# Three loads, a table and a rotation put in another order in a fused SSM and SwiGLU kernel

## The chip, the cores and the metric

The kernel runs on one core of a Trainium2 chip. A core has five engines with an instruction stream each: TensorE (PE in the profile; PEld is its weight load), VectorE (DVE), ScalarE (ACT), GpSimd (POOL) and SyncE (SP). They meet through semaphores only. Transfers between the chip's memory (DRAM) and the core's on-chip memory are made by 16 DMA engines; a transfer is issued from the queue of SP, ACT or POOL. The metric is the device time of one execution in microseconds (us), lower is better; "the time before" is the median of several runs.

## What is computed

One input x of 2048 rows by 512 columns (bf16) is normalised row by row, and the normalised x feeds two branches whose results are added to x:

```python
xn = layernorm(x)                                  # (2048, 512)
# branch A: a diagonal complex state space model
Lam_bar = exp(dt * Lam);  B_bar = ((Lam_bar - 1) / Lam)[:, None] * B
Bu = xn @ B_bar.T                                  # (2048, 512) complex
h[t] = Lam_bar * h[t-1] + Bu[t]                    # 2048 steps
yA = 2 * real(h @ C.T) + xn * Dskip
# branch B: a gated feed-forward layer, F = 1376
yB = (silu(xn @ w_gate) * (xn @ w_up)) @ w_down
out = x + yA + yB
```

## The kernel before

The 2048 rows are four chunks of 512 (`NCH`), each of four row tiles of 128 (`TPC`). Everything that TensorE multiplies needs x transposed, so a row tile is normalised in `xall` (the last chunk in `xn_end`) and transposed into `xnT`, for the first two row tiles on TensorE (`xT_pe`), for all others by a DMA transpose on SP's queue (`xT_dma`, L226).

The recurrence with complex coefficients is turned into a real one: the input of each chunk is rotated by an angle that grows with the time step (forward rotation, `rotation(..., False)`, L362), a real scan with decay `r_t` runs over it on VectorE (L400, eight scans a chunk), and the result is rotated back. The rotations multiply by two tables, cosine `c16` and sine `s16`, that the kernel makes itself: `table_ops` (L256) makes for each pair of the four 128-state groups the angles (`turns`), the sine's argument and the cosine's argument (`half`, on VectorE), and the two sines (`sine`, L278, on ScalarE). One rotation is six VectorE instructions over 2048 elements a row: f1 real part times cosine, f2 real part times sine, f3 imaginary part times sine, f4 their sum, f5 imaginary part times cosine, f6 the second sum. Its products lie in a pool of three buffers, `pm`, that the tables use too.

TensorE's order is fixed by the program. A head works on the first chunk's weight columns 0 to 5 row tile by row tile, as they come (`head_mm`, L635, in PSUM banks `held`, then `second`); `head_out` (L641) takes each finished pair of column groups through Silu and a copy on ScalarE, and a product on VectorE (L648). Then come column groups 6 and 7 (L433), which need the fourth weight group `wg3`, `wu3`; the first chunk's B projection (L358), which needs the transposed B (`BT`); groups 8 to 10; and for each later chunk its B projection, its gate and up products, and its output matmuls (L529, L536, L546).

VectorE's and ScalarE's side work is put in a list with prices by hand (`queue`), and `pump(us)` takes from the list after each piece of TensorE's work as much as the price allows; `need(tag)` takes until a tag is used up. So a changed price or place in the list shifts where every later side operation stands among the others. `multiply(keep)` issues the products that are waiting. `ln_rest(c)` (L612) is the later chunks' normalisation: four statistics (L182, L183), then `ve` (L191, VectorE), `rstd` (L192, a power on POOL), `nb` (L195) where ScalarE norms, and the four norms, each followed by its transpose.

The weights of the gate and the up projection are in five groups, each one transfer for the gate and one for the up (L112). Groups 0 to 2 are issued at the start from SP and ACT. `wg3` and `wu3` are issued from ACT behind the last `rstd_act` of the first chunk (L687, L688). `load_mid` (L135) follows on SP behind the first chunk's last transpose: the second chunk's x, eight transposes of B, the fifth weight group. `load_late` (L147) comes on SP behind the second chunk's transposes: `wu_last`, x of the third and fourth chunk, the down weights `wd_sb`. Later on SP: eight transposes of C (`CT`, L819), the third chunk's transposes, and L827, which copies x of the first three chunks to the output in DRAM; POOL adds the results onto it (L513, L557).

`params_a`, `params_a2` and `params_sin` (L246 to L306) make small per-state parameters on VectorE and ScalarE. `params_b` (L308) is a series of small multiplies on POOL.

Of the kernel before, what the change touches and what calls it, by code (L numbers as in the profile page):

```python
# [23 lines left out]
def kernel(  # L24
# [17 lines left out]
    nc = tc.nc  # L42
# [6 lines left out]
    NT = L // 128  # L49
    NCH = L // CW  # L50
    TPC = CW // 128
# [24 lines left out]
    def flat(ap3):  # L76
        return ap3.rearrange("p q j -> p (q j)")

    x_v = A_x[0].rearrange("(n p) d -> p n d", p=128)
    out_v = out[0].rearrange("(n p) d -> p n d", p=128)  # L80
    wg_v = B_w_gate.rearrange("(k p) f -> p k f", p=128)
    wu_v = B_w_up.rearrange("(k p) f -> p k f", p=128)


    xall = const.tile([128, NT, D], BF16, name="xall")
# [3 lines left out]
    wg_g, wu_g = [], []  # L89
# [6 lines left out]
    wd_sb = const.tile([128, FT, D], BF16, name="wd_sb")  # L96
# [7 lines left out]
    def wslice(groups, fi, k):  # L104
        for (a, b), t in zip(fgroups, groups):
            if a <= fi < b:
                return t[:, k, (fi - a) * 128:(fi - a) * 128 + fsz[fi]]


    def load_w1(q, tiles, view, gi):  # L110
        a, b = fgroups[gi]
        q.dma_start(out=tiles[gi][:], in_=view[:, :, a * 128:min(F, b * 128)])  # L112
# [20 lines left out]
        nc.gpsimd.dma_start(out=prm_rows[i * NQ:(i + 1) * NQ, :], in_=v.rearrange("(q j) -> q j", j=128))  # L133

    def load_mid():  # L135
        nc.sync.dma_start(out=xall[:, TPC:2 * TPC, :], in_=x_v[:, TPC:2 * TPC, :])
        for part, src in enumerate((A_B_re, A_B_im)):
            for k in range(KD):
                nc.sync.dma_start_transpose(out=BT[:, part, k, :], in_=src[:, k * 128:(k + 1) * 128])
        load_w1(nc.sync, wg_g, wg_v, 4)  # L140
        load_w1(nc.sync, wu_g, wu_v, 4)
# [3 lines left out]
        nc.gpsimd.dma_start(out=w_last[:, :, LB + LA:128], in_=wu_v[:, :, FL + LB:F])  # L145

    def load_late():  # L147
        nc.sync.dma_start(out=wu_last[:], in_=wu_v[:, :, FL:FL + LB])
        nc.sync.dma_start(out=xall[:, 2 * TPC:NT, :], in_=x_v[:, 2 * TPC:NT, :])
        nc.sync.dma_start(out=wd_sb[:, 0:nfull, :], in_=B_w_down[0:nfull * 128, :].rearrange("(k p) d -> p k d", p=128))  # L150
        if nfull < FT:
            nc.sync.dma_start(out=wd_sb[0:F - FL, nfull, :], in_=B_w_down[FL:F, :])

    nfull = F // 128
# [69 lines left out]
    def xT_dma(n):  # L224
        c, i = divmod(n, TPC)
        nc.sync.dma_start_transpose(out=xnT[:, :, n * 128:(n + 1) * 128], in_=xn_tile(c)[:, i, :])  # L226
# [62 lines left out]
    def tt(o, a, b, op):  # L289
        V.tensor_tensor(out=o, in0=a, in1=b, op=op)  # L290

    def params_sin():

        def turns(dst, shift):
            src = ws2[:]
            if shift:
                V.tensor_scalar(out=dst[:], in0=src, scalar1=shift, scalar2=None, op0=ALU.add)
                src = dst[:]
            V.tensor_scalar(out=kk[:], in0=src, scalar1=MAGIC, scalar2=MAGIC, op0=ALU.add, op1=ALU.subtract)
            tt(dst[:], src, kk[:], ALU.subtract)  # L300

        V.tensor_scalar(out=ws2[:, 1, :], in0=ws2[:, 0, :], scalar1=float(CW), scalar2=None, op0=ALU.mult)
        turns(fs1, 0.0)
        nc.scalar.activation(out=sin1[:], in_=fs1[:], func=ACT.Sin, scale=TWO_PI_LO)
        turns(fc1, 0.25)
        nc.scalar.activation(out=cos1[:], in_=fc1[:], func=ACT.Sin, scale=TWO_PI_LO)  # L306
# [55 lines left out]
    def rotation(src, dst, back):  # L362

        box = {}

        def mul(i, tab):
            t = ssm.tile([128, W], BF16, name="pm", bufs=3)
            V.tensor_tensor(out=t[:], in0=flat(src()[:, i]), in1=flat(tab[:]), op=ALU.mult)  # L368
            return t

        def f1():
            box[0] = mul(0, c16)
        def f2():
            box[1] = mul(0, s16)
        def f3():
            box[2] = mul(1, s16)
        def f4():
            V.tensor_tensor(out=flat(dst()[:, 0]), in0=box[0][:], in1=box[2][:], op=ALU.subtract if back else ALU.add)
        def f5():
            box[3] = mul(1, c16)  # L380
        def f6():
            V.tensor_tensor(out=flat(dst()[:, 1]), in0=box[3][:], in1=box[1][:], op=ALU.add if back else ALU.subtract)
        return [(1.15, f) for f in (f1, f2, f3, f4, f5, f6)]

    def ssm_ops(c):

# [49 lines left out]
    def gu_tile(c):  # L436
        if c not in gu_tiles:
            gu_tiles[c] = gut.tile([128, FT - 1, CW], BF16, name="guT")
        return gu_tiles[c]
# [125 lines left out]
    def queue(tag, ops, at=None):  # L565
        ops = [[op[0], op[1], op[2] if len(op) > 2 else None, tag] for op in ops]
        if at is None:
            backlog.extend(ops)
        else:
            backlog[at:at] = ops  # L570
# [58 lines left out]
    def head_mm(sets, fis, which, lo, hi, ks=range(KD)):  # L629

        base = lo * 128 // HALF * HALF
        for fi in fis:
            p, j = place[fi]
            for k in ks:
                nc.tensor.matmul(sets[p][which][:, j, lo * 128 - base:hi * 128 - base],  # L635
                                 lhsT=wslice((wg_g, wu_g)[which], fi, k),
                                 rhs=xnT[:, k, lo * 128:hi * 128], start=(k == 0), stop=(k == KD - 1))

    def head_out(sets, p, half):

        if half == 0:  # L641
            head_u[p] = up_p.tile([128, 2, CW], BF16, name="u2")
        cols = slice(half * HALF, (half + 1) * HALF)
        a, b = pairs[p]
        g, u = gu_tile(0)[:, a:b + 1:b - a, cols], head_u[p][:, :, cols]
        nc.scalar.activation(out=g, in_=sets[p][0][:], func=ACT.Silu)
        nc.scalar.copy(out=u, in_=sets[p][1][:])
        products.append(lambda: V.tensor_tensor(out=g, in0=g, in1=u, op=ALU.mult))  # L648
# [35 lines left out]
    rstd_act(3)  # L684
    norm_dve(3)
    xT_dma(3)
    load_w1(nc.scalar, wg_g, wg_v, 3)  # L687
    load_w1(nc.scalar, wu_g, wu_v, 3)  # L688
    load_mid()
    head_mm(held, (0, 1), 0, 1, 2, kh[0])  # L690
    head_mm(held, (0, 1), 1, 1, 2, kh[0])
# [4 lines left out]
    head_mm(held, (2, 3), 1, 0, 2)  # L696
    params_a(pp)
    params_a2()
    params_sin()
    head_mm(held, (4, 5), 0, 0, 2)  # L700
    head_mm(held, (4, 5), 1, 0, 2)
    tables = table_ops()
    stats1, norm1 = ln_rest(1, False)
    queue("tables", tables[:1])
    queue("ln1", stats1 + [(0.0, load_w_last)])
    queue("tables", tables[1:2])
    queue("ln1", norm1)
    queue("tables", tables[2:])
    second = []

    def more():
# [1 line left out]

    more()
    head_out(held, 0, 0)
    head_mm(second, pairs[0], 0, 2, 3)
    head_mm(second, pairs[0], 1, 2, 3)
    pump(GU / 2)
# [83 lines left out]
            multiply(0 if q else 1)  # L802
    fwd0, back0 = ssm_ops(0)
    stats2, norm2 = ln_rest(2, True)
    queue("ssm0", fwd0[0:2] + [(1.5, params_b)] + fwd0[2:6])
    stats3, norm3 = ln_rest(3, True)
    queue("ln2", stats2)
    queue("ssm0", fwd0[6:8])
    spread(fwd0[8:] + back0, norm2 + stats3 + norm3, "ssm0",
           ["ln2"] * len(norm2) + ["ln3"] * (len(stats3) + len(norm3)))  # L810
    queue("cf", c_ops())
# [12 lines left out]
    gateup_chunk(1)  # L824
    nc.gpsimd.dma_start(out=dsk_bc[:], in_=A_Dskip.partition_broadcast(128))
    bproj_chunk(2)
    nc.sync.dma_start(out=out[0, 0:(NT - TPC) * 128, :], in_=A_x[0, 0:(NT - TPC) * 128, :])  # L827
    queue_ssm(2)
    out_chunk(0)
    gateup_chunk(2)  # L830
# [40 lines left out]
```

## Time and profile before

| what | value |
|---|---|
| runs | 180.29, 180.37, 180.94 us; median 180.37 |
| the profiled execution's own time | 180.51 us |
| its span, from the first instruction to the last | 178.7 us |
| granted TensorE clock | 0.999 |
| DMA | 15.80 MB, mean 88 GB/s over the span |
| TensorE, matmuls of the gate and up projection (L433) | 34.6 and 34.3 us |
| TensorE, output matmuls (L529, L546) | 36.7 and 28.0 us |
| TensorE, B projection (L358) | 28.3 us |
| VectorE, scans (L400) | 24, mean 1261 ns |
| statistics of VectorE (L182), idle before them for x | 3.4 us |

The page cuts the span in 40 equal slices. A digit is a busy share in tenths:

```
PE   8989999999999999999999999999999999999992
DVE  6847998699999977999999999999999999990032
ACT  3489669988599649923966662013766600220000
DMA  5999497997366602200360000005569500162012
```

TensorE's row is full from the second slice to the last but one; the DMA engines are full in slices 2 to 8 and again later. Times in the timeline count from the span's start. A row of the timeline gives start, duration, engine, line, operation, output, inputs, shape and count, and in brackets how long the engine stood idle before it and what ended the wait. An engine with a q (SPq, ACTq) is the issue of a transfer, not the transfer.

### The profile page before, as it was taken

How to read it: one execution, taken by the hardware profiler on the slowest of the kernel's cores; microseconds unless marked ns; L12 is line 12 of the kernel's file. 1: busy time of each engine (PE TensorE's matmuls, PEld its weight loads, DVE VectorE, ACT ScalarE, POOL GpSimd, SP SyncE). 2: the span in 40 equal slices, each digit the busy share in tenths (PEclk: the TensorE clock that was granted, in tenths of full speed). 3: DMA queues.
4: the chain of work that ended last, by engine and by line, in shares of the span. 5: the costliest groups of instructions: out<-in, count | busy, mean ns of one | idle time of the engine just before them, and what ended most of it. 6: DMA issues, size and time to landing. Idle time of an engine off the chain costs nothing.

```text
span 178.7 us, 2511 instructions
## 1 busy us (share of the span) xinstructions
PE 172.8 (97%) x925; PEld 85.2 (48%) x940; DVE 152.8 (86%) x224; ACT 96.0 (54%) x172; POOL 35.7 (20%) x48
## 2 busy tenths in 40 slices
PE   8989999999999999999999999999999999999992
PEld 2879444444443444444444444444444444444752
DVE  6847998699999977999999999999999999990032
ACT  3489669988599649923966662013766600220000
POOL 6000596081500040000710000004180000150000
PEclk9999999999999999999999999999999999999999
DMA  5999497997366602200360000005569500162012
GB/s 161 302 261 158 92 199 102 254 326 157 75 75 182 231 0 59 58 4 0 39 78 0 2 4 0 0 0 59 59 94 182 82 0 0 4 86 34 0 59 59
DMA packets 30284, 15.80 MB, mean 88 GB/s; under 512 B 17904, under 2 KB 30176, under 8 KB 30240
## 3 DMA queue, kind: packets, MB, share of 16 engines
q1 hardware_dynamic: 22320, 9.97, 25.5%
q0 software_dynamic: 3536, 3.41, 14.6%
q10 hardware_dynamic: 4416, 2.26, 4.8%
q8 instruction: 7, 0.11, 0.3%
q14 instruction: 5, 0.04, 0.1%
HBM read 8.03 MB, written 5.24 MB: 74 GB/s over the span
## 4 chain that ended last, share of the span: by engine, by line
PE 78%; DVE 9%; DMA 5%; ACT 4%; issue 2%
PE ps L433 23%; PE ps L529 19%; PE ps L546 15%; PE ps L358 12%; DMA xnT<-xall 4%; PE ps L635 4%; DVE pm L368 3%; PE ps L536 2%; DVE g L400 2%; DVE stats L182 2%; DMA xall<-in_A_x_dram 1%; ACT u L448 1%; PE ps L473 1%; ACT guT L447 1%; PE ps L484 1%
## 5 line engine op out<-in xcount | busy, mean ns | idle before, releaser
L529 PE MATMUL ps<-wd_sb,guT 128*128 128x512 bf16 (+2 forms) x177 | 36.7, 355 | 0.2
L433 PE MATMUL ps<-xnT,wg 128*128 128x512 bf16 x134 | 34.6, 379 | 0.2
L433 PE MATMUL ps<-xnT,wu 128*128 128x512 bf16 x133 | 34.3, 379 | 0.1
L400 DVE TENSOR_TENSOR_SCAN g<-r_t,car,u 128x512 bf16<-128x512 f32 x24 | 28.7, 1261 | 0.0
L358 PE MATMUL ps<-xnT,BT 128*128 128x512 bf16 x126 | 28.3, 379 | 0.4 <-DMA xnT<-xall 0.3
L546 PE MATMUL ps<-CF,wt 128*128 128x512 bf16 (+2 forms) x141 | 28.0, 355 | 0.2
L557 POOL DMA_DIRECT2D out_dram<-res x12 | 10.6, 1048 | 76.4 <-ACT res L556 76.4
L529 PEld LDWEIGHTS <-guT 128*128 128x128 bf16 x180 | 16.9, 98 | 18.0
L447 ACT ACTIVATE guT<-ps 128x512 bf16<-128x512 f32 x34 | 20.4, 601 | 5.8 <-PE ps L433 5.7
L448 ACT CAST u<-ps 128x512 bf16<-128x512 f32 x34 | 20.1, 590 | 6.4 <-PE ps L433 6.4
L360 ACT CAST u<-ps 128x512 bf16<-128x512 f32 x32 | 18.2, 589 | 7.3 <-PE ps L358 7.3
L556 ACT CAST res<-ps 128x512 bf16<-128x512 f32 x12 | 6.7, 594 | 28.1 <-PE ps L546 27.0
L433 PEld LDWEIGHTS <-wu 128*128 128x128 bf16 x136 | 13.3, 98 | 16.0
L433 PEld LDWEIGHTS <-wg 128*128 128x128 bf16 x136 | 13.3, 98 | 15.8
L546 PEld LDWEIGHTS <-wt 128*128 128x128 bf16 x144 | 13.4, 98 | 14.4 <-DVE CF L344 0.4
L358 PEld LDWEIGHTS <-BT 128*128 128x128 bf16 x128 | 12.4, 98 | 15.8 <-issue 0.8
L549 DVE TENSOR_TENSOR res<-ps,xn_end 128x512 bf16<-128x512 f32 (+2 forms) x6 | 3.0, 514 | 11.9 <-PE ps L546 11.9
L192 POOL TENSOR_TENSOR rstd<-ve,neg_half 128x4 f32<-128x4 f32 x3 | 5.3, 1760 | 37.0 <-DVE ve L191 37.0
L182 DVE BATCH_NORM_STATS2 stats<-xall 128x6 f32<-128x512 bf16 x14 | 9.5, 678 | 3.4 <-DMA xall<-in_A_x_dram 3.4
L452 DVE TENSOR_TENSOR guT<-guT,u 128x1024 bf16<-128x1024 bf16 x17 | 11.4, 675 | 0.0
L368 DVE TENSOR_TENSOR pm<-u,c 128x2048 bf16<-128x2048 bf16 x8 | 9.8, 1222 | 1.5 <-ACT c L278 1.4
L368 DVE TENSOR_TENSOR pm<-g,c 128x2048 bf16<-128x2048 bf16 x8 | 9.7, 1215 | 0.1
(114 smaller groups left out, 194.2 us busy)
## 6 DMA issues: line engine op xcount, KB each, us to landing
out_dram<-in_A_x_dram SPq DMA_DIRECT2D x1, 1536.0 KB, 6.9
out_dram<-res POOLq DMA_DIRECT2D x12, 128.0 KB, 3.1
out_dram<-xall POOLq DMA_DIRECT2D x3, 512.0 KB, 9.3
wd_sb<-in_B_w_down_dram SPq DMA_DIRECT2D x1, 1280.0 KB, 9.9
wu<-in_B_w_up_dram ACTq DMA_DIRECT2D x4, 256.0 KB, 4.5
xall<-in_A_x_dram SPq DMA_DIRECT2D x1, 1024.0 KB, 6.7
wg<-in_B_w_gate_dram ACTq DMA_DIRECT2D x3, 256.0 KB, 4.7
wg<-in_B_w_gate_dram SPq DMA_DIRECT2D x2, 256.0 KB, 4.0
```

The source lines that it names most:

```text
L182: nc.vector.bn_stats(out=stats[:, n, :], in_=xall[:, n, :])
L358: nc.tensor.matmul(ps[:], lhsT=BT[:, part, k, q * 128:(q + 1) * 128], rhs=xnT[:, k, c * CW:(c + 1) * CW], start=(k == 0), stop=(k == KD - 1))
L360: nc.scalar.copy(out=u_tiles[c][:, part, q, :], in_=ps[:])
L368: V.tensor_tensor(out=t[:], in0=flat(src()[:, i]), in1=flat(tab[:]), op=ALU.mult)
L400: V.tensor_tensor_scan(out=g()[:, part, q, :], data0=r_t[:, q:q + 1].to_broadcast([128, CW]), data1=u_tiles[c][:, part, q, :], initial=ini ...
L433: nc.tensor.matmul(ps[:fs, lo:hi], lhsT=wslice(groups, fi, k), rhs=xnT[:, k, c * CW + lo:c * CW + hi], start=(k == 0), stop=(k == KD - 1))
L447: nc.scalar.activation(out=guT[:fs, fi, :], in_=psg[:fs], func=ACT.Silu)
L448: nc.scalar.copy(out=u_pair[c][:fs, fi % 2, :], in_=psu[:fs])
L452: products.append(lambda: V.tensor_tensor(out=g, in0=g, in1=u, op=ALU.mult))
L529: nc.tensor.matmul(o[:], lhsT=gu_tiles[c][:, fi, i * 128:(i + 1) * 128], rhs=wd_sb[:, fi, lo:hi], start=(fi == 0), stop=False)
L546: nc.tensor.matmul(o[:], lhsT=w_tiles[c][:, part, q, i * 128:(i + 1) * 128], rhs=CF[:, part, q, lo:hi], start=False, stop=(c > 0 and part ...
L557: nc.gpsimd.dma_start(out=out_v[:, n, :], in_=res[:], accum_op=ALU.add)
```

## The change

- `wg3` and `wu3` are issued from POOL instead of ACT. Ahead of them VectorE sets two elements of `wg3` to zero, behind the first chunk's last norm; as the load overwrites them, POOL has to wait for it.
- The second chunk's x is issued from POOL behind those two, instead of from SP ahead of B's transposes.
- In `load_late` x of the third and fourth chunk goes ahead of `wu_last`, and the large part of `wd_sb` is two transfers.
- A forward rotation issues f2, f3, f1, f4, f5, f6; the backward one is unchanged.
- `params_sin` moves behind the first `head_out`. On VectorE its instructions stay where they were, on ScalarE its two sines come behind that Silu and copy.
- In the list, the sine's argument of the first state pair (`tables[1]`) comes ahead of the second chunk's statistics, and the cosine's (`tables[2]`) ahead of its norms.
- In the list, the third chunk's statistics come after f4 of the first chunk's rotation, instead of after f6. The price of `params_b` goes from 1.5 to 0.1.
- The copy of x to the output is two transfers. As the list is used up sooner, the fourth chunk's transposes stand ahead of it on SP.

```diff
     def load_mid():
-        nc.sync.dma_start(out=xall[:, TPC:2 * TPC, :], in_=x_v[:, TPC:2 * TPC, :])
         for part, src in enumerate((A_B_re, A_B_im)):
...
     def load_late():
+        nc.sync.dma_start(out=xall[:, 2 * TPC:NT, :], in_=x_v[:, 2 * TPC:NT, :])
         nc.sync.dma_start(out=wu_last[:], in_=wu_v[:, :, FL:FL + LB])
-        nc.sync.dma_start(out=xall[:, 2 * TPC:NT, :], in_=x_v[:, 2 * TPC:NT, :])
-        nc.sync.dma_start(out=wd_sb[:, 0:nfull, :], in_=B_w_down[0:nfull * 128, :].rearrange("(k p) d -> p k d", p=128))
+        wd_v = B_w_down[0:nfull * 128, :].rearrange("(k p) d -> p k d", p=128)
+        for a, b in ((0, 5), (5, nfull)):
+            nc.sync.dma_start(out=wd_sb[:, a:b, :], in_=wd_v[:, a:b, :])
...
-        return [(1.15, f) for f in (f1, f2, f3, f4, f5, f6)]
+        return [(1.15, f) for f in ((f1, f2, f3, f4, f5, f6) if back else (f2, f3, f1, f4, f5, f6))]
...
     xT_dma(3)
-    load_w1(nc.scalar, wg_g, wg_v, 3)
-    load_w1(nc.scalar, wu_g, wu_v, 3)
+    nc.vector.memset(wg_g[3][:, 0, 0:2], 0.0)
+    load_w1(nc.gpsimd, wg_g, wg_v, 3)
+    load_w1(nc.gpsimd, wu_g, wu_v, 3)
+    nc.gpsimd.dma_start(out=xall[:, TPC:2 * TPC, :], in_=x_v[:, TPC:2 * TPC, :])
     load_mid()
...
     params_a2()
-    params_sin()
     head_mm(held, (4, 5), 0, 0, 2)
...
-    queue("tables", tables[:1])
+    queue("tables", tables[:2])
     queue("ln1", stats1 + [(0.0, load_w_last)])
-    queue("tables", tables[1:2])
+    queue("tables", tables[2:3])
     queue("ln1", norm1)
-    queue("tables", tables[2:])
+    queue("tables", tables[3:])
...
     head_out(held, 0, 0)
+    params_sin()
     head_mm(second, pairs[0], 0, 2, 3)
...
-    queue("ssm0", fwd0[0:2] + [(1.5, params_b)] + fwd0[2:6])
+    queue("ssm0", fwd0[0:2] + [(0.1, params_b)] + fwd0[2:4])
     stats3, norm3 = ln_rest(3, True)
     queue("ln2", stats2)
-    queue("ssm0", fwd0[6:8])
+    queue("ssm0", fwd0[4:8])
...
-    nc.sync.dma_start(out=out[0, 0:(NT - TPC) * 128, :], in_=A_x[0, 0:(NT - TPC) * 128, :])
+    for a, b in ((0, TPC * 128), (TPC * 128, (NT - TPC) * 128)):
+        nc.sync.dma_start(out=out[0, a:b, :], in_=A_x[0, a:b, :])
```

## The prediction

> **What bounds the kernel now.** First the page's busy shares.
>
> ```profile
> span 178.7 us, 2511 instructions
> PE 172.8 (97%) x925; PEld 85.2 (48%) x940; DVE 152.8 (86%) x224; ACT 96.0 (54%) x172; POOL 35.7 (20%) x48
> ```
>
> TensorE (PE) has work almost throughout; the profiled execution took 180.51 us, 1.8 us of it outside the span. So a change that removes no matmul can gain only what PE stands still. Next, therefore, PE's own waits:
>
> ```profile
> PE ps L635 <- DMA xnT<-xall: 0.8, 1, 0.8
> PE ps L358 <- DMA xnT<-xall: 0.3, 1, 0.3
> ```
>
> Both are for transposed x. The waits understate the loss, since a matmul's modelled end runs past the slot in which the next can start. So I took slots from the timeline. First stretch:
>
> ```profile
> 7.83 2.62 SPq L226 DMA_TRANSPOSE xnT<-xall  x2
> 8.17 0.41 ACTq L112 DMA_DIRECT2D wg<-in_B_w_gate_dram  x1
> 8.62 0.68 ACTq L112 DMA_DIRECT2D wu<-in_B_w_up_dram  x1
> ...
> 10.20 1.04 PE L635 MATMUL ps<-xnT,wu 128*128 128x256 bf16 x8
> ...
> 10.50 0.58 SPq L136 DMA_DIRECT2D xall<-in_A_x_dram  x1
> ...
> 11.99 0.62 PE L635 MATMUL ps<-xnT,wg 128*128 128x128 bf16 x8 [0.75 <-DMA xnT<-xall]
> ```
>
> The eight 256-column matmuls of 9.33 hand over at 10.20: 0.109 each. The eight of 10.20 are thus through at 11.07, and the next start at 11.99: **0.92 lost**. They wait for row tile 2, whose transpose was issued at 7.83 and landed 4.1 later. What the DMA engines did meanwhile, in the queue view of 10.5 to 11.7:
>
> ```profile
> q10 hardware_dynamic: 643, 0.32, 110.5%
> q1 hardware_dynamic: 32, 0.00, 1.6%
> ```
>
> q10 is ScalarE's queue, q1 SyncE's: the fourth weight group, issued at 8.17 and 8.62, had the engines nearly to itself while PE waited for q1. Second stretch:
>
> ```profile
> 48.59 0.14 DVE L195 SCALAR_TENSOR_TENSOR nb<-mv,rstd 128x4 f32<-128x4 f32 x1
> ...
> 48.76 0.81 ACT L205 ACTIVATE xall<-xall,nb,rstd 128x512 bf16<-128x512 bf16 x1 [1.20 <-DVE nb L195]
> ...
> 56.27 1.03 PE L433 MATMUL ps<-xnT,wu 128*128 128x512 bf16 x4
> ...
> 57.62 4.69 PE L358 MATMUL ps<-xnT,BT 128*128 128x512 bf16 x20 [0.32 <-DMA xnT<-xall]
> ```
>
> 512 columns take 0.216 a slot (32 in 6.9 in stage L358), so the four of 56.27 are through at 57.13: **0.49 lost** at 57.62. This goes back through the transpose and the norms on ScalarE to `nb` of the third chunk on VectorE, late because VectorE was idle earlier:
>
> ```profile
> 14.59 0.69 DVE L182 BATCH_NORM_STATS2 stats<-xall 128x6 f32<-128x512 bf16 x1 [2.88 <-DMA xall<-in_A_x_dram]
> ...
> 21.23 0.85 POOL L144 DMA_DIRECT2D w_last<-in_B_w_gate_dram  x1
> 21.87 1.12 DVE L200 TENSOR_SCALAR xall<-xall,mv,rstd 128x512 bf16<-128x512 bf16 x3
> 22.09 0.80 POOL L145 DMA_DIRECT2D w_last<-in_B_w_up_dram  x1
> ...
> 33.95 1.23 DVE L368 TENSOR_TENSOR pm<-u,c 128x2048 bf16<-128x2048 bf16 x1 [1.36 <-ACT c L278]
> ```
>
> From 58 on PE is closed up. At most some 1.4 us is to be had, plus a few hundredths between stages.
>
> **The change, part by part.** *Hold and POOL issue.* The memset (row: 128x4 memset, 0.06) follows the last first-chunk norm, which ends at 8.81, so POOL issues from about 8.9. The nearest rows, `w_last` with as many rows per transfer, took 0.85 and 0.80 each; the far ones, the skip stores, 1.30 to 1.65. I take 0.85, the same kind of load: wg3 at 8.9, wu3 at 9.75, the second chunk's x at 10.6. From issue to landing 256 KB took 3.5 to 4.9 on the other queues; POOL's 512 KB accumulating stores took 5.6 to 10.8. SP's 512 KB x took 4.1, and POOL's small `w_last` (3.4) stood 1.2 over SP's `wu_last` (2.2). So wg3 is there by 14, wu3 by 15.5 (PE wants them at 17.32 and 18.18, less 0.92), and x at 10.6+4.1+1.2 = 15.9; bounds 14.7 and 21.4.
>
> *Tile 2 and 3 transposes.* Without q10's load a transpose lands 2.45 (the last chunk's four) to 2.8 (the median of BT's imaginary half) after issue: tile 2 at 10.3 to 10.65, wanted at 11.07. The 0.92 goes. PE then wants tile 3 sixteen plus sixteen short matmuls later, at 11.07+32x0.056 = 12.86. Issued at 9.25, it lands at 11.7 clean. Beside POOL's 128 KB of `w_last`, the last BT transpose took 3.6: 12.9, a wait of 0.04. I take none, since POOL's first data can come only about 1.9 after 8.9 (an estimate from `w_last`: issued 21.23, the engines' software queue first busy about 23.1).
>
> *ScalarE* is rid of 0.41+0.68 of issuing; `dt_t` (9.34) starts when prm is there, about 9.05, and the table load ends at 11.0, not 11.28. With the two small sines (0.21, 0.19) put behind the first Silu and copy, those run 11.0 to 12.06. This matters: the second pair reuses their banks at 11.07+0.88 = 11.95 and 12.39. At the old times (12.08, 12.55) it would have cost 0.16.
>
> *VectorE.* The half of the sine table (0.69+1.23) moves ahead of the second chunk's statistics and fills the 2.88 idle. But as built, five products stand ahead of the first statistics, and the fifth needs ScalarE's copy of the fifth pair, about 16.3 (before, less 0.2). So: product to 16.65, four statistics at 0.80 to 19.9, product 20.3, half of the cosine table (0.69+0.72+1.22) to 23.05, product 23.7, four norms at 0.37 to 25.2. x at 15.9 is hidden behind that product with 0.75 to spare. Before, the norms ran 21.87 to 23.91, so **this chain is later**, not earlier. SP loses one issue (0.58), passes BT and the fifth weights by 23.1, and issues the four transposes at 24.1 and 1.3 apart: the last at 28.0 instead of 27.74, landing at 30.5 to 30.8 (2.45 to 2.8). PE wants it at 32.09-0.92 = 31.17. The row of 3.6 would make it 31.6; I charge 0.1 for that. The last BT transpose came at 24.91 when wanted at 24.87; it is issued 0.6 or more sooner and no longer beside `w_last`: nothing.
>
> *Sine first.* The sine is ready at 32.97 before, 0.92 sooner now as it follows PE's pace on ScalarE: the rotation starts at 32.05 instead of 33.95, and the cosine multiply, third, never waits. With f5 and f6 behind the third chunk's statistics, `ve` comes at about 40.7 (45.14) and `nb`, behind f5, f6 and three scans, at 46.7 (48.59). The norms stand one weight pair sooner on ScalarE, 1.67 apart: the last ends about 52.5, its transpose lands at 55.0; PE wants it at 57.13-0.92 = 56.2. The 0.49 goes. x of chunks three and four, issued behind the transposes at 29.4 without `wu_last` (0.57) ahead, lands 6.7 later at 36.1; the statistics want it at 37.4.
>
> *The rest.* wd_sb in two: one more SP issue (0.58), so CT's transposes end at 46.9 instead of 46.3; the next transpose wants SP at 47.4. The output copy in two: it now stands behind the fourth chunk's transposes, issued about 71 instead of 56.30, landed (6.9) by 79; POOL's first accumulation onto it is at 86.18. Were that gone, it would still be off PE's path. params_b's smaller price only moves the order. What is late next: the fourth chunk's last transpose landed at 73.98 with PE there at 74.3; PE being 1.4 sooner, it must be 1.1 sooner; VectorE is 1.9 ahead since the rotation, so nothing, and the C factors behind them likewise.
>
> *Sum*, against 180.51: -0.92 -0.49 +0.10 = -1.31, so 179.2. The runs' median, 180.37, is 0.14 below that execution: **179.1 us**.
>
> **Rivals.** (A) *The second chunk's transposes take over.* For: the chain above is the later one by its own rows, margin 0.4 to 0.7. If VectorE reaches the norms 1.4 us later than I reckon, PE waits about 0.9 at stage L358: gain 0.5, 179.9. Against: every step before them has a row.
>
> (B) *Tile 2 stays late.* The third weight group's second half, still on ScalarE's queue, landed only at 9.84. If that and not the fourth group held the transpose, the 0.92 stays and only 0.49 goes: 179.9. Against: 110% of q10 between 10.5 and 11.7, when the third group had landed.
>
> (C) *POOL's loads come late (slower side).* If POOL's issues stall beside VectorE, which is busy 8.9 to 11.4 and 12.1 to 14.3, wg3 goes out about 11.5, wu3 14.4 to 15.5, x at 16.5, landing near 20. The statistics begin 3.3 later than 16.7, the last transpose lands at 33.8: PE starts the second B projection 1.7 later than before, and the third chunk, 3 later on VectorE, gains nothing: 182.1. It decides when x lands after 16.7 + (32.1-30.8) = 18.0. For: POOL's small multiplies took 0.20 to 1.21 for the same shape. Against: L145 took 0.80 beside three norms of VectorE, no longer than the 0.86 of the output stores that POOL issues singly.
> By the Trainium skill, SBUF — State Buffer, section "SBUF: two separate sides", a VectorE operation in a two-port mode locks GpSimd out of writing descriptors, and a POOL-issued DMA of 620 ns becomes 3100. By that figure the three issues would cost an estimated 7.4 us more and x would land beyond 22. The trace does not bear it out at 21.87 to 22.99, but shows it beside no table arithmetic.
>
> **How the numbers follow.** Forecast 0.58, A 0.15, B 0.13, C 0.12, the rest scattered (0.02). About 0.5% (0.9 us) is what a measurement of this kernel tells from no change: faster is under 179.47. The forecast is nearly all there; A and B fall within; C is slower. Faster 0.60, same 0.28, slower 0.12. Low end 178.6: 1.4 plus the few tenths between stages near 73 and 75 (0.09 and 0.10) and the spread of the runs. High end 180.7 takes in A and B; C's 182.1 stays out.
>
> **What would show it.** Right: no PE wait near 11, tile 2 landed under 11; the last transpose of chunk two before PE; the first rotation near 32; no PE wait at stage L358 for chunk three. Wrong: statistics of chunk two idle on x past 16.7 (C), a wait of PE for `xnT` near 31 (A) or still near 11 (B).

## The result and the profile after

| what | before | after |
|---|---|---|
| runs, median (lowest to highest), us | 180.81 (180.29 to 183.2), 6 runs | 182.05 (181.59 to 182.61), 6 runs |
| ratio to before, 95% interval | | 1.0072 [1.0045, 1.0099] |
| the profiled execution's own time, us | 180.51 | 182.61 |
| its span, us | 178.7 | 180.8 |

Ratios, here and below, compare fast runs alone, and the medians below are theirs: of the six runs before, 183.2 stays out (the other five have a median of 180.69), and so do four, four and one of twelve runs in three kernels below (183.2 to 184.6 us, at a granted clock of 0.987 to 0.991).

The change made the kernel slower by 0.7%. Forecast was 179.1.

TensorE's waits after, from the view of waits; the columns are the sum in us, the number of waits and the longest:

```profile
PE ps L359 <- DMA xnT<-xall: 1.8, 1, 1.8
PE ps L359 <- DMA BT<-in_A_B_re_dram: 0.6, 1, 0.6
PE ps L636 <- DMA xnT<-xall: 0.5, 1, 0.5
```

Three new waits stand where two were, all of them for transfers. Their places, from the timeline after:

```profile
8.15 2.62 SPq L227 DMA_TRANSPOSE xnT<-xall  x2
9.45 0.82 POOL L112 DMA_DIRECT2D wg<-in_B_w_gate_dram  x1 [5.32 <-DVE prm L248]
10.27 0.77 POOL L112 DMA_DIRECT2D wu<-in_B_w_up_dram  x1
11.04 0.75 POOL L691 DMA_DIRECT2D xall<-in_A_x_dram  x1
11.43 0.61 PE L636 MATMUL ps<-xnT,wg 128*128 128x128 bf16 x8
13.89 0.61 PE L636 MATMUL ps<-xnT,wg 128*128 128x128 bf16 x8 [0.51 <-DMA xnT<-xall]
20.54 0.69 DVE L183 BATCH_NORM_STATS2 stats<-xall 128x6 f32<-128x512 bf16 x1 [3.49 <-DMA xall<-in_A_x_dram]
22.05 2.18 PE L359 MATMUL ps<-xnT,BT 128*128 128x512 bf16 x8 [0.58 <-DMA BT<-in_A_B_re_dram]
35.12 1.24 PE L359 MATMUL ps<-xnT,BT 128*128 128x512 bf16 x5 [1.83 <-DMA xnT<-xall]
```

Row tile 2 is on time: its matmuls start at 11.43 with no wait. Row tile 3 is not (13.89). VectorE stands 3.49 for the second chunk's x and begins its statistics at 20.54, 3.9 later than the prediction had them; the transposed B comes late (22.05); and the second chunk's transposes, which follow those statistics, hold TensorE until 35.12. Counted in slots as in the prediction, TensorE loses 0.67 at tile 3, 0.74 and 0.28 for B, 1.99 at chunk two: 3.68, where before lost 0.92, 0.09 (at 24.7) and 0.49. That is 2.2 more; the two profiled executions differ by 2.1 (the one after was 0.36 later from the start and won some 0.4 back behind the third chunk). How long the transfers took, from the queue view of after between 10.2 and 11.1 (the last column is us from issue to landing):

```profile
xall<-in_A_x_dram POOLq DMA_DIRECT2D x1, 512.0 KB, 9.5
wg<-in_B_w_gate_dram POOLq DMA_DIRECT2D x1, 256.0 KB, 4.2
wu<-in_B_w_up_dram POOLq DMA_DIRECT2D x1, 256.0 KB, 6.4
xnT<-xall SPq DMA_TRANSPOSE x1, 4.3
BT<-in_A_B_re_dram SPq DMA_TRANSPOSE x1, 9.7
```

GpSimd issued at its usual pace (0.82, 0.77, 0.75). What took long came after the issue, and for everything that was in flight: x 9.5 where before it took 4.1, B's first transpose 9.7 where it took 5.4. In the view of windows of after (the window and its length; TensorE, weight load, VectorE, ScalarE, GpSimd busy; then clock, share of the 16 DMA engines, GB/s):

```profile
15.00:16.00 1.00, 1.00 (x18) 0.97 (x16) 0.66 (x2) 1.00 (x4) 0.00 (x0) 1.00 0.92 62
17.00:18.00 1.00, 1.00 (x9) 0.67 (x7) 0.04 (x1) 0.72 (x2) 0.00 (x0) 1.00 0.52 101
```

The DMA engines are shown 0.92 and 0.52 busy and move 62 and 101 GB/s; before, at 12 to 13, they moved 293.

### The profile page after: what moved, and what is told of

Same layout as the page of the kernel before. It is cut to its first block, busy times and chain, and to the rows that moved or that the text cites. A ratio compares the mean times of both kernels' runs of the same rounds, so it can differ in the third digit from the quotient of the medians.

```text
span 180.8 us, 2531 instructions
## 1 busy us (share of the span) xinstructions
PE 173.8 (96%) x940; PEld 85.2 (47%) x940; DVE 153.4 (85%) x225; ACT 96.8 (54%) x172; POOL 35.9 (20%) x51
## 4 chain that ended last, share of the span: by engine, by line
PE 79%; DMA 10%; DVE 7%; ACT 1%; issue 1%; POOL 1%; DVEq 0%
PE ps L434 29%; PE ps L530 19%; PE ps L547 15%; PE ps L359 12%; DMA xall<-in_A_x_dram 5%; DMA wu<-in_B_w_up_dram 3%; PE ps L537 2%; DMA xnT<-xall 2%; PE ps L485 1%; DVE stats L183 1%; DVE pm L275 1%; DVE xall L201 1%; PE ps L474 1%; DVE pm L274 1%; ACT L118 0%
## 5 line engine op out<-in xcount | busy, mean ns | idle before, releaser
L434 PE MATMUL ps<-xnT,wu 128*128 128x512 bf16 x136 | 34.9, 379 | 0.0
L361 ACT CAST u<-ps 128x512 bf16<-128x512 f32 x32 | 18.5, 585 | 8.6 <-PE ps L359 8.5
```

The costliest lines, as they stand in the source:

```text
L361: nc.scalar.copy(out=u_tiles[c][:, part, q, :], in_=ps[:])
L434: nc.tensor.matmul(ps[:fs, lo:hi], lhsT=wslice(groups, fi, k), rhs=xnT[:, k, c * CW + lo:c * CW + hi], start=(k == 0), stop=(k == KD - 1))
```

## The experiments

At first three theories stood. COLLISION: the three loads, now on another queue, travel at the same time as SP's transposes, and each draws the other out. POOL SLOW: loads on GpSimd's queue are slow of themselves. ORDER: the reordered lists lose the time, not the loads. Times are medians, with the ratio to before on the same chip; waits of TensorE are counted in slots. A transfer's time is from its issue to its landing. All diffs are against the changed kernel unless said otherwise.

**The loads back, and the loads alone.** The first kernel is the changed one with the three loads as before; the second is the kernel before with the three loads moved and nothing else.

```diff
+        nc.sync.dma_start(out=xall[:, TPC:2 * TPC, :], in_=x_v[:, TPC:2 * TPC, :])
...
-    nc.vector.memset(wg_g[3][:, 0, 0:2], 0.0)
-    load_w1(nc.gpsimd, wg_g, wg_v, 3)
-    load_w1(nc.gpsimd, wu_g, wu_v, 3)
-    nc.gpsimd.dma_start(out=xall[:, TPC:2 * TPC, :], in_=x_v[:, TPC:2 * TPC, :])
+    load_w1(nc.scalar, wg_g, wg_v, 3)
+    load_w1(nc.scalar, wu_g, wu_v, 3)
```

> The changed kernel with its three loads as before (wg3 and wu3 from ScalarE, the second chunk's x on SP ahead of B's transposes), all else as changed. Theory COLLISION (POOL's three loads and B's transposes share the DMA engines and slow each other) and theory POOL SLOW (what POOL issues comes late whatever else is in flight) both put the whole loss on the loads: x lands about 14.6, B's first half before TensorE asks for it, no wait near 21 or 33, the 0.9 near 11 is back, the 0.49 near 57 is gone; time 0.3 to 0.6 us under the kernel before. Theory ORDER (the loss comes from the new order of VectorE's work, the five products ahead of the statistics) expects a wait of 1 us or more near 32 even so, and a time over the kernel before.

> The kernel before with only the three loads moved to POOL behind the memset. COLLISION and POOL SLOW: x lands near 20, B's first half after 20, TensorE waits about 0.5 near 13, about 1 at 21 and 1 to 2 near 32, and the 0.49 near 57 stays or grows: 1 to 2.5 us over the kernel before. ORDER: no more than 0.3 us from the kernel before, since the statistics stand ahead of the products here.

Loads back: 180.47, 0.999 of before ([0.9972, 1.0007]), no clear difference, where 0.3 to 0.6 us less was expected. Only the wait for tile 2 is there again, 1.25 in this execution (0.92 before); none at 21, 33 or 57. Loads alone: 185.4, 1.0262 [1.0223, 1.03], 4.7 us over before, where 1 to 2.5 were expected: 0.82 lost near 13, 1.0 in three waits for B, 2.54 at 32.8, and 1.77 at 60.4 for the third chunk. So the loss is in the loads and ORDER falls; the rest of the change even hides some of it. The timeline of the first kernel shows what the rest does by itself:

```profile
33.91 2.36 DVE L370 TENSOR_TENSOR pm<-u,s 128x2048 bf16<-128x2048 bf16 x2 [0.44 <-ACT s L280]
48.28 0.14 DVE L197 SCALAR_TENSOR_TENSOR nb<-mv,rstd 128x4 f32<-128x4 f32 x1
58.03 1.24 PE L360 MATMUL ps<-xnT,BT 128*128 128x512 bf16 x5
```

The rotation starts no sooner than before (33.95) and `nb` only 0.3 sooner (48.59), but TensorE finds the third chunk ready: its last transpose landed at 57.40 (before 57.48), and TensorE came at 58.03, 0.9 later than before.

**One load at a time.** x back on SP; the fourth weight group back on ScalarE; and all three on GpSimd, with B's transposes held until the second chunk's first statistics.

```diff
+        nc.sync.dma_start(out=xall[:, TPC:2 * TPC, :], in_=x_v[:, TPC:2 * TPC, :])
...
-    nc.gpsimd.dma_start(out=xall[:, TPC:2 * TPC, :], in_=x_v[:, TPC:2 * TPC, :])
```

> The changed kernel with only the second chunk's x back on SP ahead of B's transposes; wg3 and wu3 stay on POOL. COLLISION: wg3 and wu3 (0.5 MB) still overlap the third row tile's transpose, so a wait of 0.4 to 0.7 near 13 stays, but x goes through SP's queue ahead of B and B's first half meets an empty POOL queue: x lands near 15, no wait near 21 and under 0.3 near 32; 0.5 to 1.0 us under the kernel before. POOL SLOW: the same for x, but wu3 lands near 16.6 as it did in the changed kernel.

```diff
-    nc.vector.memset(wg_g[3][:, 0, 0:2], 0.0)
-    load_w1(nc.gpsimd, wg_g, wg_v, 3)
-    load_w1(nc.gpsimd, wu_g, wu_v, 3)
+    load_w1(nc.scalar, wg_g, wg_v, 3)
+    load_w1(nc.scalar, wu_g, wu_v, 3)
+    nc.vector.memset(xall[:, TPC, 0:2], 0.0)
```

> The changed kernel with wg3 and wu3 back on ScalarE where they were; the second chunk's x alone on POOL, held by a two-element memset of its first row tile at the same place. Theory VOLUME (the harm is the megabyte that POOL puts beside the transposes): x alone, 0.5 MB, lands within 6 us, by 15 to 16, B's first half by 19, no wait near 21, under 0.5 near 32; the 0.9 near 11 is back; within 0.5 us of the kernel before. Theory POOL QUEUE (one POOL load beside transposes is enough): x lands past 18, a wait of over 1 us near 32.

```diff
-    load_mid()
...
-    queue("ln1", stats1 + [(0.0, load_w_last)])
+    def bt_hold():
+        nc.vector.memset(BT[:, 0, 0, 0:2], 0.0)
+        load_mid()
+    queue("ln1", stats1[:1] + [(0.0, bt_hold)] + stats1[1:] + [(0.0, load_w_last)])
```

> The changed kernel with B's transposes held on SP by a two-element memset of BT behind the first statistics of the second chunk, so that nothing is transposed while POOL's loads are in flight, except the third row tile. COLLISION: x, issued near 11, lands by 15 to 16 (4 to 5 us) instead of 20.5, wu3 by 15. POOL SLOW: x still lands near 20, wu3 near 16.6. Either way B comes later than TensorE wants it, by several us, and the kernel is slower; only the landings are read.

x on SP: 181.04, 1.0008 [0.9992, 1.0025], not the 0.5 to 1.0 us under before that was expected; x takes 6.5, B is in time, TensorE loses 1.00 at 13.15 (tile 3 still late) and 0.47 at 32. B held: 186.21 in a single run, since B itself is then late; x, on GpSimd's queue, takes 6.4. So B's company costs x 3.0 of its 9.5, as far as one run each can tell. Weights on ScalarE with x alone on GpSimd: 188.55, 1.0433 [1.0394, 1.0473], the worst of the three. Its transfers, in the queue view from 9.0 to 9.8 (of the two transposes the median):

```profile
xall<-in_A_x_dram POOLq DMA_DIRECT2D x1, 512.0 KB, 9.3
wg<-in_B_w_gate_dram ACTq DMA_DIRECT2D x1, 256.0 KB, 3.6
wu<-in_B_w_up_dram ACTq DMA_DIRECT2D x1, 256.0 KB, 8.3
xnT<-xall SPq DMA_TRANSPOSE x2, 7.5
```

Tile 3's transpose, issued at 9.73, landed at 20.63, and TensorE stood 6.36. That looked like GpSimd's queue at fault, with one load enough; but `wu3` on ScalarE's queue took 8.3 there too. It took the next runs to part the two readings. Not all of the 188.55 is waiting: the granted clock falls to 0.50 during the long stop and stays there until 25.3, so that TensorE also works at half its clock for 4.6 us. The trace shows 0.50 in the same way, for some microseconds behind a stop of over 6, in the kernels of 188.93 and 187.33 below; with B held it reads 0.50 for 3.4 us from the last of the waits for B on.

**The same loads on ScalarE's and on SP's queue.** Here the theories are VOLUME (so many bytes at once) and POOL QUEUE (a load on GpSimd's queue). Weights on ScalarE behind the first `head_out`, x on SP; all three behind the first `head_out`; all three on SP ahead of B. The edit of the first:

```diff
+        nc.sync.dma_start(out=xall[:, TPC:2 * TPC, :], in_=x_v[:, TPC:2 * TPC, :])
...
-    nc.vector.memset(wg_g[3][:, 0, 0:2], 0.0)
-    load_w1(nc.gpsimd, wg_g, wg_v, 3)
-    load_w1(nc.gpsimd, wu_g, wu_v, 3)
-    nc.gpsimd.dma_start(out=xall[:, TPC:2 * TPC, :], in_=x_v[:, TPC:2 * TPC, :])
...
     head_out(held, 0, 0)
     params_sin()
+    load_w1(nc.scalar, wg_g, wg_v, 3)
+    load_w1(nc.scalar, wu_g, wu_v, 3)
```

> The changed kernel with nothing of the loads on POOL: x on SP ahead of B as before, wg3 and wu3 from ScalarE, but behind the first Silu and copy (about 12.2) instead of at 8.2. Both theories: tile 2 lands under 11 and the 0.9 near 11 goes, tile 3 lands under 12.9 as nothing is in flight beside it, x lands near 14.6. VOLUME: wg3 and wu3 then overlap x and B's first transposes, so B's first half lands past 20 and a wait of 0.3 to 1 appears near 21. POOL QUEUE: B comes as before, no wait near 21, and the kernel is 0.8 to 1.3 us faster than before.

> The changed kernel with all three loads from ScalarE's queue behind the first Silu and copy (about 12.2 to 13.5) and none on POOL; B's transposes go out from about 10.5 as in the changed kernel. VOLUME: the same megabyte beside B's transposes, so x lands 8 us or more after its issue, past 20.5, B's first half past 20, and the time is as the changed kernel's or worse. POOL QUEUE: x lands 4 to 5 us after its issue, near 18, and B's first half before 20: under 1 us over the kernel before.

> The changed kernel with all three loads on SP's queue, behind the third row tile's transpose and ahead of B: wg3, wu3, x, then B; nothing moves on another queue beside a transpose. Both theories: no wait near 11 or 13, wu3 near 14, x near 15.5. B's transposes are issued 0.9 us later than in the kernel before, so its second half lands near 25.5 where TensorE wants it at 24: a wait of 0.5 to 1.2 near 24. Time 0.2 to 0.9 us under the kernel before.

The first two measured something else. 181.99 (1.0075 [1.006, 1.0091]) and 188.93 (1.045 [1.0421, 1.0478]): the issue on ScalarE's queue stood and waited for an unrelated transfer, and Silu behind it. ScalarE's row in the first:

```profile
15.36 0.37 ACTq L112 DMA_DIRECT2D wu<-in_B_w_up_dram  x1
15.78 0.60 ACT L648 ACTIVATE guT<-ps 128x512 bf16<-128x512 f32 x1 [3.49 <-DMA xall<-in_A_x_dram]
```

`wu3` could only go when x had landed (15.33), though nothing in the program joins the two. The transfers share a few semaphores in turn, and the one that `wu3` was given had x before it. Still, tile 3 took 2.48 in both. All on SP: 181.56, 1.0049 [1.0028, 1.0069], over before and not 0.2 to 0.9 us under it, with no wait at 11, 13, 21, 32 or 57 and one of 1.95 at 23.9 for B's last transpose. Issued at 22.19, it took 3.84, beside `w_last` on GpSimd's queue.

**Earlier on ScalarE, and w_last off GpSimd.** Now ScalarE's issues stand between `dt_t` and `r_t`, where no semaphore holds the weights up. The first kernel has x on SP, the third all three loads on ScalarE; the second is the all-SP kernel with `w_last` behind the fifth weight group on SP. The edit of the first, without the lines that it shares with the one above:

```diff
-    load_mid()
...
     params_a(pp)
+    load_w1(nc.scalar, wg_g, wg_v, 3)
+    load_w1(nc.scalar, wu_g, wu_v, 3)
+    load_mid()
     params_a2()
```

> After, with the second chunk's x back on SP ahead of B's transposes and the fourth weight group back on ScalarE's queue, but later than before: between dt_t and r_t, about 9.3 and 10.3, so that the second row tile's transpose (issued about 8) still goes ahead of it. No load is on POOL's queue early. POOL QUEUE (what slowed after is a load on POOL's queue beside SP's transposes): tile 2 lands under 11, tile 3 by 12.9, x 4 to 5 after its issue, BT's real half by 19.5, last transpose of chunk two before PE; no wait over 0.4 at 13, 21 or 33. ScalarE's first Silu comes about 0.5 later for the two issues, which may cost up to 0.4 at the reused banks near 12. Against before's 180.5 execution: -0.92 -0.49 +0.1 to +0.4 = 179.2 to 179.6, ratio 0.993 to 0.996. ANY SECOND QUEUE (a load on any queue beside the transposes slows them as POOL's did): tile 3 at 13.5 or later, BT at 20 or later, waits of 0.5 or more at 13 and at 21, x over 6; 181 or more.

> The kernel with all three loads on SP ahead of B's transposes (181.56), with the two small w_last loads moved from POOL to SP behind the fifth weight group. POOL QUEUE: in that kernel the last B transpose took 3.84 from issue to landing beside w_last on POOL, and PE waited 1.95 for it. Without POOL's load it takes 2.5 to 2.8, so the wait falls by 1.0 to 1.3, to 0.7 to 0.95: 180.3 to 180.6. ANY SECOND QUEUE / no effect of w_last: the wait stays at 1.7 to 2.0 and the time at 181.4 to 181.7.

> After, with the same three loads issued from ScalarE's queue between dt_t and r_t instead of from POOL's: the weights at about 9.3 and 9.9, x when its semaphore is free, about the landing of tile 3's transpose (12 to 13), so ScalarE's r_t and first Silu come 1 to 2 late and PE waits up to 2 near 13 to 14 for a bank; the time is no guide (181 to 184). To read is the time from issue to landing beside the same transposes. POOL QUEUE: wg3 and wu3 land 3.5 to 5 after issue, x 4 to 5 after its issue, tile 3 by 13, BT's real half by 20 at its own issue rate of about 1.3 a piece. ANY SECOND QUEUE: wu3 and x 6.4 and 8 or more, tile 3 at 13.8 or later, BT 7 or more after issue.

Weights on ScalarE: 180.86, 1.0007 [0.9991, 1.0022]. Tile 3, from its queue view between 10.5 and 11.0, and TensorE behind it in the timeline:

```profile
xall<-in_A_x_dram SPq DMA_DIRECT2D x1, 512.0 KB, 6.5
xnT<-xall SPq DMA_TRANSPOSE x1, 5.4
```
```profile
15.09 0.61 PE L637 MATMUL ps<-xnT,wg 128*128 128x128 bf16 x8 [1.47 <-DMA xnT<-xall]
```

5.4 beside ScalarE's load, worse than 4.3 to 4.6 beside GpSimd's so far; x took 6.5 in both. So for tile 3 the queue's name does not matter, and POOL QUEUE falls there. All three on ScalarE: 187.33, 1.0365 [1.0338, 1.0393], with tile 3 at 6.65, and x, which had to wait for tile 3's landing, issued at 16.12 and landed 4.5 later. `w_last` on SP: 182.11, 1.0077 [1.0058, 1.0097]. B's last transpose went from 3.84 to 2.82, as expected of `w_last`'s company, and its own wait fell to 0.50. The time missed all the same: 1.17 came at 32.7, where two more issues of 0.51 on SP stand ahead of the second chunk's transposes, so that gain was spent on SP's queue; and 0.75 came at 20.8 for B's real half, ahead of `w_last`, which this run does not explain.

**x alone, and the weights held longer.** COMPANY says that the queue does not matter, only what else is in flight when a transfer goes. First x alone on GpSimd's queue beside B, released when tile 3 has landed (weights on ScalarE as above). Then the kernel with x on SP, its weights held until tile 2 has landed transposed; then the same with x in two halves.

```diff
+    nc.gpsimd.tensor_copy(out=xall[:, TPC, 0:2], in_=xnT[:, 0, 3 * 128:3 * 128 + 2])
+    nc.gpsimd.dma_start(out=xall[:, TPC:2 * TPC, :], in_=x_v[:, TPC:2 * TPC, :])
```

> The kernel with three loads on ScalarE's queue (187.33), with x on GpSimd's queue instead, released when row tile 3 has landed transposed; the fourth weight group stays on ScalarE. So x travels beside B's transposes and beside nothing else. On ScalarE's queue, released at 16.12 by the same event, it took 4.5 from issue to landing. POOL QUEUE (GpSimd's queue itself is slow beside transposes): 7 or more, and B's transposes beside it 6 or more from issue to landing. COMPANY (the queue does not matter; a transfer is drawn out by what else is in flight when it is issued): 4.5 to 5.5, B's transposes within 5.5. Tile 3 again lands at 14.5 to 16.1 in both, beside the weights on ScalarE.

```diff
-    nc.vector.memset(wg_g[3][:, 0, 0:2], 0.0)
+    nc.gpsimd.tensor_copy(out=wg_g[3][:, 0, 0:2], in_=xnT[:, 0, 2 * 128:2 * 128 + 2])
```

> The kernel with x back on SP and the weights on GpSimd (181.04), with the weights held until row tile 2 has landed transposed (about 10.6) instead of until the first chunk's last norm (8.9); their data then start at about 12.4. COMPANY: tile 3, issued about 9.5, is out of the way by then and lands at 11.9 to 12.3; the wait of 1.00 near 13 goes. The weights land at about 14.7 and 16.5 to 17 (wanted at 16.4 and 17.3), x at 17.0 to 17.8; a wait of 0 to 0.3 near 16.5 and of up to 0.7 near 32. 179.6 to 180.4, ratio 0.994 to 0.998. POOL QUEUE: with the weights later beside all of B's transposes, B's real half lands past 21 and PE waits 0.5 or more there; wu3 8 or more after its issue, so that PE waits 1 or more for it near 17: 181 or more.

```diff
-        nc.sync.dma_start(out=xall[:, TPC:2 * TPC, :], in_=x_v[:, TPC:2 * TPC, :])
+        for i in (TPC, TPC + 2):
+            nc.sync.dma_start(out=xall[:, i:i + 2, :], in_=x_v[:, i:i + 2, :])
```

> As the kernel before it, with the second chunk's x in two transfers of two row tiles each on SP, so that VectorE's statistics can start on the first half. COMPANY: first half lands at 15.5 to 16.6, before VectorE wants it at 16.65; the second by 17.8, before 18.3. The wait near 32 goes; B's transposes are issued 0.6 later, which may cost up to 0.4 at 24: 179.4 to 180.2. POOL QUEUE: as for the kernel before it, 181 or more.

x alone (182.62 in a single run), in the queue view from 16.0 to 21.0:

```profile
xall<-in_A_x_dram POOLq DMA_DIRECT2D x1, 512.0 KB, 4.7
BT<-in_A_B_im_dram SPq DMA_TRANSPOSE x4, 3.8
```

4.7 on GpSimd's queue against 4.5 on ScalarE's, released by the same event beside the same transposes: GpSimd's queue is not slow. Weights held longer: 180.39, 0.9983 [0.9967, 0.9998], the only one of all these kernels whose interval stays below 1, and by 0.2%, less than the 0.5% that the prediction took for the least that can be told from no change; the forecast of 179.6 to 180.4 is met at its edge. Tile 3 took 2.48 and x 4.8; there is no wait at 13, but 0.31 and 0.27 near 17 for the weights and 0.60 at 24.5 for B's last transpose, again beside `w_last`. With x in halves (181.0, 1.0012 [0.9993, 1.0032]) that last one grew to 2.41, as B went 0.5 later and met `w_last`.

**The hold between the two.** The last pair issues the weights between the two times seen, behind the product `ws` on VectorE, and moves `w_last`: right behind `wu3`, or held until B's last transpose has landed.

```diff
     params_a2()
+    nc.vector.memset(wg_g[3][:, 0, 0:2], 0.0)
+    load_w1(nc.gpsimd, wg_g, wg_v, 3)
+    load_w1(nc.gpsimd, wu_g, wu_v, 3)
+    load_w_last()
...
-    queue("ln1", stats1 + [(0.0, load_w_last)])
+    queue("ln1", stats1)
```

> The kernel with x on SP and the weights held on GpSimd until row tile 2 has landed (180.39), with two things moved: the weights' hold ends behind the phase product ws on VectorE, so they are issued at about 10.1 instead of 11.4, and w_last follows them on GpSimd at once, about 11.7. COMPANY: tile 3 still lands by 12.2, the weights at 15.3 to 16.2 and 16.5 to 17.3 (the waits of 0.31 and 0.27 go); the last B transpose, no longer issued beside w_last, takes 2.5 to 2.9 instead of 3.9, and its wait of 0.60 near 24.5 goes; B's real half lands up to 0.8 later (by 20.8, just in time). 179.3 to 179.9, ratio 0.991 to 0.996. If w_last's 1024 small pieces draw out x or B's real half instead, PE waits 0.5 or more near 21 or 32: 180.4 or more.

> As the kernel before it, but w_last is held on GpSimd until B's last transpose has landed, about 24, so that it is issued at about 24.6 and 25.4 and lands by 29.6 (wanted at 31.4). COMPANY: waits at 16.5, 17.5 and 24.5 go as there, B's real half is as before; instead the second chunk's transposes, issued 24 to 28, travel beside it and may land up to 1 later (31.2 before, wanted at about 31.7): a wait of 0 to 0.5 near 32. 179.3 to 180.1, ratio 0.991 to 0.998.

181.4 (1.0017 [0.9996, 1.0038]) and 180.92 (1.0017 [1.0, 1.0034]): both expectations missed, above all at one place. B's last transpose took 2.9 and 2.8 without `w_last`, as expected, but the hold was too short: tile 3 took 5.67 and 4.52, and TensorE lost 2.05 and 0.91 there. (Later waits, 0.36 in the first and 0.45 in the second, come on top.) This pair shows the mechanism closest. The queue view from 10.45 to 11.55, first of the kernel held longer, then of the first of this pair (packets, MB, share of the engines):

```profile
q1 hardware_dynamic: 544, 0.13, 59.2%
xnT<-xall SPq DMA_TRANSPOSE x1, 2.5
```
```profile
q1 hardware_dynamic: 512, 0.13, 57.5%
xnT<-xall SPq DMA_TRANSPOSE x1, 5.7
```

In both all 0.13 MB of tile 3 have gone by 11.55. In the one all 544 packets have, and it lands at 11.86. In the other 32 packets of 4 bytes are left, GpSimd's load starts at 11.66, and in 11.66 to 13.0 the same view reads:

```profile
q0 software_dynamic: 47, 0.18, 103.2%
q1 hardware_dynamic: 23, 0.00, 2.1%
```

The load (q0) has the engines, and the transpose lands at 15.22, 3.7 after 11.55. The prediction's own row of q1, "32, 0.00" beside ScalarE's q10 between 10.5 and 11.7, was the same thing at tile 2: its 512 other packets had gone by 10.5.

| row tile 3's transpose | us from issue to landing |
|---|---|
| no load of another queue started before it landed (six kernels) | 2.47 to 2.48 |
| GpSimd's weights beside it (after, and five kernels) | 4.28, 4.37, 4.42, 4.52, 4.55, 5.67 |
| ScalarE's weights issued ahead of it and of x (before, and loads back) | 3.88, 4.54 |
| ScalarE's weights issued beside it (x on SP, on ScalarE later, on GpSimd later) | 5.45, 6.65, 6.30 |
| ScalarE's weights and GpSimd's x beside it | 10.9 |

Nothing lies between 2.48 and 3.88. In seven of the twelve kernels with a load beside it, tile 3 landed 0.24 to 0.37 after one of the two weight transfers had (after: 13.85, `wg3` 13.61; with ScalarE's weights and x on SP: 15.05, `wu3` 14.69), as if it had to let that load through first. In the last pair it landed ahead of both (15.22 and 14.09, `wg3` 15.64 and 15.92). x goes by the same rule: 4.1 to 4.8 with B's transposes alone, or with the weights well ahead of it or starting behind it, 5.2 behind the weights on SP's own queue, 6.2 to 6.5 with the weights beside it, 9.3 to 9.5 with the weights ahead and B beside it.

## Why the prediction was wrong

**Of the two gains one came as forecast.** Tile 2 landed at 10.66, inside the 10.3 to 10.65 forecast but for 0.01, and the 0.92 was gone. The 0.49 was gone too, but not for the reason given: TensorE starts the third chunk without a wait because it comes later itself, in after (60.16, its last transpose landed at 58.29, 0.8 later than before) and with the loads back (58.03, landed at 57.40, 0.1 sooner, in an execution that issued tile 2 0.56 later than before did). The step under it failed: "the rotation starts at 32.05" was 34.46, and 33.91 with the loads back; `nb`, forecast at 46.7, came at 48.85 and 48.28, the last transpose not at 55.0. With the loads back the wait went with 0.6 to spare where the prediction had 1.2, and TensorE was itself later than the forecast 56.2. That this wait went is luck as far as the forecast goes. The reordered lists do help the third chunk: its last transpose landed at 62.28 with the loads alone, where TensorE lost 1.77, and at 56.72 with the weights held longer. Whether a transpose that lands at 57.4 holds a TensorE that comes at 56.2, no run shows: none came so early.

**"I take none" at tile 3: 0.67.** This is the step that failed first. Two things stood behind it: that POOL's first data come about 1.9 after the issue (an estimate from `w_last`), and that 3.6, the row beside `w_last`, is the worst. POOL issued at 9.45, not 8.9, and its data came 1.57 later, at 11.02, about 1.0 before a clean landing at 12.05. That was enough: 4.28, not 2.45 and not 3.6. The prediction's own numbers had this already: 8.9 and 1.9 make 10.8, ahead of its clean landing at 11.7, so a late first byte was no reason to charge nothing. The collision which the change took away from tile 2 it gave to tile 3.

**x at 15.9: 20.52.** The largest miss. The term added 1.2 to SP's 4.1 for a different queue; the measured surcharge is not the queue's (4.7 against 4.5 by itself) but the company's: 9.5 with `wg3` and `wu3` ahead and B's transposes beside it. The prediction had moved x to where SP's order no longer kept it ahead of B, and counted that as a gain for SP (0.58 sooner) only. x lay within its bounds of 14.7 and 21.4, and past the 18.0 at which it named the sign to turn.

**"Nothing" for B: 1.02. 0.10 for the second chunk's transposes: 1.99.** Both follow. B's real half, its first transpose issued 0.3 sooner than before, landed at 20.52 to 22.50 in place of 16.52 to 19.42. The second chunk's statistics began at 20.54 in place of the forecast 16.65, and its last transpose landed at 35.03, 4.2 past the forecast 30.8; TensorE came there at 33.13, 2.0 past the forecast 31.17 (1.6 for the waits that it already had, the rest from its later start), and started at 35.12: 1.99.

**Sum.** -0.92 -0.49, -0.09 for the wait that before had at B's last transpose, +0.67 +1.02 +1.99: +2.2 between the two executions, and 1.36 between the medians, 182.05 and 180.69. The profiled execution of after is its slowest.

**The rivals.** C had the time (182.1 against 182.05) and the place: VectorE idle on x past 16.7. It had the wrong mechanism, so the time is luck. Its issues were to stall; they took 0.82, 0.77 and 0.75 at 9.45 to 11.79, with VectorE 0.93 busy in the windows 10 to 11 and 11 to 12, fp32 table work beside the third of them. By the Trainium skill, SBUF — State Buffer, section "SBUF: two separate sides", those issues could have been locked out; the trace does not show it here. A's wait at chunk two came, but as the end of x's chain, with 1.99 instead of 0.9. B fell: tile 2 was on time.

**What stays open.** Why 32 packets wait for microseconds. The Trainium skill, DMA: Bandwidth & Descriptors, section "Queues, rings and completion order", says that a DMA engine takes the queues that have work in turn, a whole packet of several descriptors at a time. If a load's piece for one engine counts as one turn there, `wg3` is 64 of the 4 KB packets on 16 engines, 4 each, at 0.5 (44 of the 47 packets above are of that size, in 1.34 us), an estimated 2.0 for a turn; 3.7 would be nearly two turns, `wg3`'s and `wu3`'s. That fits in size; no run tests it, and `wg3` itself landed only behind tile 3 there. A rival is in the traces: of that transpose's sixteen completion signals eleven had come by 13.47, 1.8 after the load's first data, fifteen by 14.37, and one alone at 15.22, with a 16 KB instruction fetch (one packet, queue q8) of 0.94 started at 13.08. With B held, fifteen of x's signals had come by 16.24 and the last at 17.53, behind such a fetch of 1.33 at 13.50, and the share of the DMA engines reads 0.06, one in sixteen, at 16 to 17. So the last part of some of these times may be one engine that a fetch left behind; no run takes that apart. Nor do the runs tell how much of x's 9.5 is the weights' and how much B's beyond the one difference of 3.0.

## What to carry to other kernels

A load that is held back to let a transfer through is only out of the way if its data start after that transfer has landed, last packets included; count from its first data (on GpSimd's queue here 1.5 to 2.9 after the issue), not from its end. Before a load leaves a queue, ask what the order of that queue protected it from: x ahead of B on SP took 6.5, not 9.5. And where a change takes a wait away from one transfer, look which one the same traffic meets next; here tile 2's 0.92 became tile 3's 0.67.

## What was not expected of the hardware

- A DMA transpose next to a load of another queue finishes late although its data are through: 544 packets and 2.48 without the load, 512 packets by the same time and 5.67 with it.
- The queue of the load hardly matters: 4.28 to 5.67 beside GpSimd's, 3.88 to 6.65 beside ScalarE's, for the same 0.5 MB.
- A long stop costs TensorE more than the stop: with the weights on ScalarE and x on GpSimd its granted clock read 0.50 from 18.5 to 25.3, and TensorE had work again from 20.67 on.
- An issue on ScalarE can stand for another queue's transfer: `wu3` went 0.03 after x had landed, and ScalarE stood 3.49.
